# Linear attention and a hardswish layer on one core: the second chunk's features in two transfers, and three constants of the planner

## The chip, the core and the metric

The kernel runs on one core of a Trainium2 chip. The metric is device time of one execution in microseconds (us); of several runs the median is given. The engines are TensorE (PE; its weight loads are PEld), VectorE (DVE), ScalarE (ACT), GpSimd (POOL) and SyncE (SP), which here only issues transfers.

## The reference

```python
# r, k, v, w: (4, 8, 768, 48), u: (8, 48)
for t in range(S):
    cur = einsum('bhd,bhe->bhde', u * k_t, v_t)
    y[:, :, t] = einsum('bhd,bhde->bhe', r_t, state + cur)
    state = w_t[..., None] * state + einsum('bhd,bhe->bhde', k_t, v_t)
x = y.transpose(0, 2, 1, 3).reshape(3072, 384)
h = x @ w_in                          # 384 x 2048, given in float64
g = h * clip(h + 3, 0, 6) / 6
out = g @ w_out                       # 2048 x 384, given in float64
```

## The kernel before, in words

**Work.** The sequence is cut into 24 chunks of 128 tokens, and six blocks of four chunks. The recurrence of a chunk is turned into small matrix products; each finished block of 512 tokens then goes through the two large products. Block 0 does most of its large products directly; blocks 1 to 5 use a seven-product scheme for both of them.

**Steps of chunk i.** `feat{i}` fetches r, k and w side by side as one tile of 112 x 1545 values (`load_feat`), `tok{i}` fetches v. On DVE, `back{i}` scans w backwards (L372) and takes a reciprocal; `fore{i}` scans w forwards (L381); `K{i}` is k times the first scan (L392), `R{i}` is r times the second (L396), `own{i}` is r times k (L405). The two scans need only w. PE then does `dot{i}` (L415), `score{i}` (L440), `turn{i}` (a transpose, L456) and `kv{i}` (L536); ACT copies what `turn`, `dot` and `kv` left (`turned`, `sum`, `kvs`) and builds a diagonal (`diag0`, `diag1`, L431). `above{i}` merges the scores on DVE (L447), and `mid`, `decb`, `state`, `decay` carry the state on. In block 0, `first{i}` reads the last pair of heads on PE (L514, L523), `third{i}` copies it on ACT, `read{i}` does the rest on PE (L584, L514, L523), and `leave{i}` copies the result out on ACT. In later blocks `begin{i}` and `read{i}` take these places.

**Weights.** They arrive as float64. `fetch{j}` (j = 0 to 15, the first eight for w_in) brings 768 KB; ACT does `low{j}` and `whole{j}` (L340, L344), DVE does `shift{j}`, `join{j}` and `full{j}` (L349, L354, L359). `up0.f.c0` is a product of block 0 with w_in (L639) on two chunks, followed by `ramp` on ACT (L629) and `gate` on DVE (L650); `down0.c.q` is a product with w_out (L658) and needs `full{8+q}`. The steps `sin` and `sout` (L700, L712) make the sums of weights that the seven-product scheme needs; `up1.…` and `down1.…` are that scheme's products (L740, L791).

**What sets the order.** Every step is given to a planner (`plan.add`) with its engine, an assumed duration, the steps that it must follow, a due time ("key") and the buffers that it holds until named steps are done. The planner writes one fixed order for each engine from these; each engine then works through its order, and waits where something is late. `LAG` sets how long ahead of a block its chunks are due, `CONV` the due time of the first weight conversion and the distance from one to the next, `SUMS` the same for the sums. Three buffers hold features (`feat_in`), three hold raw weights (`bits`), two hold `more` and one holds `y_ps`, in which `kv`, `first` and `read` write.

**Start.** Until the first `up0.0.0` the planner puts "spins" on PE between steps: products of an identity whose result nobody reads (L1130), so many as fit into the time that it assumes PE would be idle.

Of the kernel before, what the change touches and what calls it, by code (L numbers as in the profile page):

```python
# [24 lines left out]
GBC = 3  # L25


LAG = 6.1
AHEAD = -3.5
LEAD = 2.5  # L30
BEHIND = (-1, -1, -1, 0, 6, 7)
# [1 line left out]
OWN = 0.07  # L33
SOLO = (0, 2, 3, 4, 5)
EARLY = 7
START = (-118.3, -135.2, -24.4, -60.3, -5.9, 13.2)
CONV = (-100.6, 7.2)
UP = (-68.7, 1.2, -9.3, 6.3)
SUMS = (52.1, 1.4)
LEAST = 2.0 ** -60  # L40

WORD_MIN, WORD_MAX = 1.125 * 2.0 ** -15, 1.875 * 2.0 ** 16
# [145 lines left out]
def fast_path(tc, feat, tok, wflat, ub, ug, moe_w_in, moe_w_out, out, flag, n_chunks):  # L188
# [5 lines left out]
    nc = tc.nc  # L194
# [13 lines left out]
    f64 = moe_w_in.dtype != F32  # L208

    with ExitStack() as ctx:  # L210
# [8 lines left out]
        chunk_of = [(i // NSEQ * 2 + i % 2) * n_chunks + i % NSEQ // 2 for i in range(NT)]  # L219
# [7 lines left out]
        plan = Plan()  # L227
        st = [dict() for _ in range(NT)]
# [8 lines left out]
        back = const.tile([PR, 2 * P, HL + 1], F32, name="back")  # L237
        starts = [const.tile([PR, 2 * P, HL + 1], F32, name=f"start_{i}") for i in range(2)]
        states = [const.tile([PR, P, D], F32, name=f"state_{i}") for i in range(2)]
        u_col = const.tile([PR, P, 2], F32, name="u_col")  # L240
# [37 lines left out]
        n = P * L  # L278
# [3 lines left out]

        def load_feat(i):
            a = io.tile([PR, nf], F32, name="feat_in")
            if i == 0:
                nc.sync.dma_start(out=a[:, 2 * n:], in_=feat[chunk_of[i], :, 2 * n:])
                nc.scalar.dma_start(out=u_col, in_=ug)
            else:
                nc.sync.dma_start(out=a, in_=feat[chunk_of[i]])
            st[i].update(a=a, r=a[:, :n].rearrange("q (x t) -> q x t", t=HL),  # L290
                         k=a[:, n:2 * n].rearrange("q (x t) -> q x t", t=HL), w=a[:, 2 * n:])

        def load_rest():
            nc.sync.dma_start(out=st[0]["a"][:, :2 * n], in_=feat[chunk_of[0], :, :2 * n])

        def load_u():
            nc.sync.dma_start(out=u_bc, in_=ub.to_broadcast([128, HD]))
# [569 lines left out]
        def do(fn, *args):  # L867
            return lambda: fn(*args)
# [5 lines left out]
        def when(i):  # L874

            bk, c = divmod(i, BC)
            return BASE[bk] - LAG - (BASE[bk] - BASE[bk - 1]) / BC * (BC - 1 - c) if bk else -99.0

# [6 lines left out]
        def scored(i):  # L885
            return f"score{i}" if i <= BC else f"read{i - 1}"

        def turned_by(i):
            return f"turn{i}" if i <= BC + 1 else f"begin{i - 2}"
# [4 lines left out]
        for i in range(NT):  # L894
            t = when(i)
            k = START[i] if i < len(START) else when(i - 2) - AHEAD
            first, last = is_first(i), is_last(i)
            dve = i < EARLY
            behind = [f"fetch{BEHIND[i]}"] if i < len(BEHIND) and BEHIND[i] >= 0 else []
            plan.add(f"feat{i}", "SP", 0.45 if i else 1.15, do(load_feat, i), behind + [f"feat{i - 1}"] * (i > 0) + ["later"] * (i == 1), k - 20, kb=690 if i else 231,  # L900
                     hold=[("feat", [f"K{i}", f"R{i}"] + [f"own{i}"] * (i < BY_PE))])
            plan.add(f"tok{i}", "SP", 0.45, do(load_tok, i), behind + [f"feat{i}"] * (i > 1) + ["later"] * (i < 2), k - 19.9, kb=197,
                     hold=[("tok", [f"read{i}"])])
            if i >= BY_PE:
                plan.add(f"rkt{i}", "SP", 0.45, do(load_rk, i), behind + [f"feat{i}"] * (i > 0), k - 19.8, kb=393,
                         hold=[("rk_in", [f"own{i}"])])
            plan.add(f"back{i}", "DVE", 1.4, do(back_scan, i), [f"feat{i}"] + [f"fore{i - 2}"] * (i > 1) + [f"back{i - 1}"] * (i > 0), k,
                     [("E", [f"K{i}", f"least{i}"])], port=True)
            plan.add(f"K{i}", "DVE" if dve else "POOL", 0.66 if dve else 1.32, do(make_k, i), [f"back{i}", f"least{i}"] + [f"K{i - 1}"] * (i > 0) + ["later"] * (i == 0),
                     k + 0.1, [("K", [scored(i), turned_by(i)])], port=True)  # L910
            plan.add(f"fore{i}", "DVE", 1.23, do(fore_scan, i), [f"back{i}"] + [f"fore{i - 1}"] * (i > 0), k + 0.2,
                     [("W", [scored(i), f"read{i}" if i < BC else f"begin{i}"])], port=True)
            plan.add(f"R{i}", "DVE" if dve else "POOL", 0.66 if dve else 1.32, do(make_r, i), [f"fore{i}"], k + 0.3,
                     port=True)
            plan.add(f"least{i}", "ACT", 0.2, do(least, i), [f"back{i}"], k + 0.2)
            if i < BY_PE:
                plan.add(f"own{i}", "DVE", 0.66, do(own, i), [f"feat{i}"] + ["later"] * (i == 0) + [f"own{i - 1}"] * (i > 0), k + OWN,
                         [("rk", [f"dot{i}"])], port=True)
                plan.add(f"dot{i}", "PE", 0.85, do(own_dot, i), [f"own{i}"], k + OWN, [("ps", [f"sum{i}"])])
                plan.add(f"sum{i}", "ACT", 0.22, do(own_sum, i), [f"dot{i}"], k + OWN, [("dg", [f"diag1{i}"])])  # L920
            else:
                plan.add(f"own{i}", "POOL", 2.0, do(own, i), [f"rkt{i}", "u"] + [f"own{i - 1}"] * (i > 0), k + 0.4,
                         [("rk", [f"sum{i}"])], port=True)
                plan.add(f"sum{i}", "DVE", 0.54, do(own_sum, i), [f"own{i}"], k + 0.5, [("dg", [f"diag1{i}"])])
# [3 lines left out]
            t = k + 1 if i < len(START) else t  # L928
# [52 lines left out]
                                 [f"leave{i - 1}", f"leave{i}"], when(i) - 50, kb=1, dmas=3)  # L981

        plan.add("u", "SP", 0.45, load_u, ["fetch3"], -60.0, kb=197)
        plan.add("later", "SP", 0.45, load_rest, ["feat0"], key=-999.0, kb=459)

        for j in range(len(pairs)):
            t = CONV[0] + j * CONV[1]
            plan.add(f"fetch{j}", "SP", 0.45, do(fetch, j), ["later"] * (j == 0), key=t - 20, kb=768 if f64 else 384,
                     hold=[("bits", [f"low{j}", f"join{j}"])] if f64 else ())
            if f64:  # L990
                plan.add(f"low{j}", "ACT", 0.9, do(low_scaled, j), [f"fetch{j}"], t, [("more", [f"full{j}"])])
                plan.add(f"whole{j}", "ACT", 0.84, do(low_whole, j), [f"low{j}"], t)
                plan.add(f"shift{j}", "DVE", 0.56, do(high_shift, j), [f"fetch{j}"], t, [("top", [f"full{j}"])], port=True)
                plan.add(f"join{j}", "DVE", 0.96, do(high_join, j), [f"shift{j}"], t, port=True)
                plan.add(f"full{j}", "DVE", 0.94, do(high_low, j), [f"join{j}", f"whole{j}"], t, port=True)
# [5 lines left out]
        for x, (c0, c1) in enumerate(parts):  # L1001
            m = c1 - c0
            for f in range(NFC):
                k = UP[2 * x] + f * UP[2 * x + 1]
# [7 lines left out]
        for c in classic:  # L1012
            for q in range(HF):
                k = D0 + c * D0 / BC + q * 1.29
# [9 lines left out]
        for n_, (s_, q) in enumerate((s_, q) for s_ in (1, 2, 4, 3) for q in range(0, HF, 2)):  # L1024
# [9 lines left out]
            if s_ in (2, 4) and q == 0:  # L1034
                before += [f"sin{s_ // 2}.{HF - 2}"]
            plan.add(f"sin{s_}.{q}", "DVE", 0.36, do(sum_in, s_, q), before, SUMS[0] + n_ * SUMS[1] / 4, hold, port=True)
        for n_, (t_, x) in enumerate((t_, x) for t_ in (1, 2, 4, 3) for x in range(2)):
# [3 lines left out]
            if t_ == 1 and x == 0:  # L1041
                before += [f"{ready}{len(pairs) - 1}"]
            plan.add(f"sout{t_}.{x}", "DVE", 0.95, do(sum_out, t_, x), before, SUMS[0] + 4 * SUMS[1] + n_ * SUMS[1] / 2,
                     [("bits", ["end"])] * (t_ != 3 and x == 0), port=True)
# [3 lines left out]
        for bk in range(NB):  # L1048
            K = BASE[bk]
# [67 lines left out]
        for k, (which, j) in enumerate(vets):  # L1117
            i = 8 + k // 2
# [255 lines left out]
def kernel(  # L1374
# [25 lines left out]
    flags = ctx.enter_context(tc.tile_pool(name="flags", bufs=1))  # L1400
    flag = flags.tile([1, 1], I32, name="flag")
    fast_path(tc, feat, tok, wflat, ub, ug, moe_w_in, moe_w_out, out, flag, n_chunks)
    bad = nc.values_load(flag[0:1, 0:1], min_val=0, max_val=128)
    with tc.If(bad > 0):
# [65 lines left out]
```

## Time and profile before

| | us |
|---|---|
| median of 6 runs | 574.91 (571.45 to 576.36) |
| the profiled execution | 571.62 |
| its span | 569.9 |
| first `up0.0.0` on PE | 32.0 |
| last product on PE ends | 564.6 |

The span is the time between the first and the last instruction that the profile has; the remaining 1.7 us of the execution lie around it. PE is busy for 558.0 us of it, DVE for 405.0, ACT for 273.6, POOL for 99.8. The 18 us that PE spent in spins count as busy. In the windows of the profile "PEclk" is the TensorE clock that was granted, as a share of full speed; in the timeline a bracket at the end of a row tells how long the engine was idle before it and which event ended that.

### The profile page before, as it was taken

The numbers are of one execution on the slowest core, as the hardware profiler recorded it, in microseconds if no ns is written. First come the engines' busy times: TensorE is split into PE (matmuls) and PEld (weight loads), VectorE is DVE, ScalarE is ACT, GpSimd is POOL, SyncE is SP. The second block draws the span as 40 slices with busy tenths as digits, with TensorE's granted clock in tenths as the row PEclk, the third lists the DMA queues.
The fourth block names the chain that finished last, engine by engine and source line by source line (L and its number), as shares of the span: only waits on it lengthen the run. The fifth ranks groups of instructions, "written<-read, shape, count | busy, mean of one in ns | idle before, by whom it ended". The sixth has DMA issues, their size and how long they took to land.

```text
span 569.9 us, 13575 instructions
## 1 busy us (share of the span) xinstructions
PE 558.0 (98%) x5636; PEld 500.9 (88%) x5636; DVE 405.0 (71%) x713; ACT 273.6 (48%) x724; POOL 99.8 (18%) x111
## 2 busy tenths in 40 slices
PE   8999899999999999999999999999999999999996
PEld 8888587689888999988999988999988999988996
DVE  7999989988687858677878767878656625255350
ACT  4688664643565633276633366633266611355100
POOL 2000000245513321223123133123122000000000
PEclk9999899999999999999999999999999999999998
DMA  8987822531613246930368360367100001000001
GB/s 273 279 276 232 266 67 64 158 110 44 181 55 99 78 125 203 252 89 12 123 214 266 98 168 8 127 205 220 41 16 2 9 1 36 29 1 1 1 15 47
DMA packets 23078, 63.98 MB, mean 112 GB/s; under 512 B 3120, under 2 KB 10352, under 8 KB 23008
## 3 DMA queue, kind: packets, MB, share of 16 engines
q1 hardware_dynamic: 22880, 63.02, 36.5%
q8 instruction: 46, 0.75, 0.6%
q14 instruction: 24, 0.20, 0.1%
q10 hardware_dynamic: 128, 0.00, 0.0%
HBM read 57.31 MB, written 4.72 MB: 109 GB/s over the span
## 4 chain that ended last, share of the span: by engine, by line
PE 94%; DVE 2%; DMA 2%; ACT 1%; issue 1%; SPq 0%; DVEq 0%; ACTq 0%
PE bankA L791 20%; PE bankA L740 18%; PE bankC L791 10%; PE bankC L740 9%; PE bankB L740 6%; PE bankB L791 5%; PE bankC L639 3%; PE bankA L639 3%; PE bankA L658 3%; PE y_ps L514 3%; PE y_ps L523 2%; PE y_ps L536 2%; PE ps L456 2%; DMA bits<-in_moe_w_in_dram 2%; PE bankB L440 2%; PE ps L415 1%
## 5 line engine op out<-in xcount | busy, mean ns | idle before, releaser
L749 ACT COPY g<-bankA 128x256 f32<-128x256 f32 x120 | 44.3, 371 | 58.7 <-PE bankA L740 56.7
L791 PE MATMUL bankA<-w_out,g 128*128 128x192 f32 x352 | 63.9, 328 | 0.0
L629 ACT ACTIVATE clip<-g,three 128x512 f32<-128x512 f32 x80 | 57.9, 723 | 7.9 <-DVE g L751 7.2
L740 PE MATMUL bankA<-xT,w_in 128*128 128x256 f32 x240 | 60.1, 382 | 0.0
L759 DVE SCALAR_TENSOR_TENSOR g<-clip,g 128x512 f32<-128x512 f32 x80 | 56.9, 712 | 2.6 <-ACT clip L629 2.4
L791 PEld LDWEIGHTS bankA<-w_out,g 128*128 128x128 f32 x352 | 57.9, 190 | 0.9
L804 ACT ACTIVATE o<-bankA 128x192 f32<-128x192 f32 x33 | 10.9, 330 | 88.8 <-PE bankA L791 88.8
L740 PEld LDWEIGHTS bankA<-xT,w_in 128*128 128x128 f32 x240 | 44.8, 190 | 6.0
L431 ACT ACTIVATE A<-eyes,dg 128x64 f32<-128x64 f32 x192 | 49.2, 336 | 0.4
L606 ACT COPY xT<-y_ps 48x256 f32<-48x256 f32 x80 | 29.3, 366 | 37.3 <-PE y_ps L523 36.4
L392 POOL TENSOR_TENSOR K<-feat_in,E 112x512 f32<-112x512 f32 x17 | 21.5, 1265 | 136.0 <-PE bankC L440 121.8
L740 PE MATMUL bankB<-xT,w_in 128*128 128x256 f32 x160 | 41.1, 379 | 0.0
L751 DVE TENSOR_TENSOR g<-bankB,g 128x256 f32<-128x256 f32 x40 | 16.9, 423 | 32.3 <-PE bankB L740 30.6
L396 POOL TENSOR_TENSOR W<-feat_in,W 112x512 f32<-112x512 f32 x17 | 23.1, 1357 | 87.2 <-DVE W L381 87.2
L751 DVE TENSOR_TENSOR g<-bankC,g 128x256 f32<-128x256 f32 x40 | 16.9, 421 | 27.3 <-PE bankC L740 27.2
L740 PEld LDWEIGHTS bankB<-xT,w_in 128*128 128x128 f32 x160 | 30.4, 190 | 4.1
L381 DVE TENSOR_TENSOR_SCAN W<-feat_in,start 112x520 f32<-112x520 f32 x24 | 30.6, 1274 | 3.1 <-PE y_ps L514 3.0
L372 DVE TENSOR_TENSOR_SCAN E<-feat_in,back 112x520 f32<-112x520 f32 x24 | 30.0, 1251 | 3.3 <-DMA feat_in<-in_feat_dram 3.1
L791 PE MATMUL bankA<-bits,g 128*128 128x192 f32 x176 | 30.3, 327 | 0.5 <-DVE o L806 0.5
L791 PE MATMUL bankB<-w_out,g 128*128 128x192 f32 x176 | 30.4, 326 | 0.0
L791 PEld LDWEIGHTS bankA<-bits,g 128*128 128x128 f32 x176 | 28.8, 190 | 0.9 <-DVE o L806 0.7
L791 PEld LDWEIGHTS bankB<-w_out,g 128*128 128x128 f32 x176 | 28.9, 190 | 0.0
(277 smaller groups left out, 1211.0 us busy)
## 6 DMA issues: line engine op xcount, KB each, us to landing
feat_in<-in_feat_dram SPq DMA_DIRECT2D x23, 675.9 KB, 5.9
bits<-in_moe_w_in_dram SPq DMA_DIRECT2D x8, 768.0 KB, 10.3
bits<-in_moe_w_out_dram SPq DMA_DIRECT2D x8, 768.0 KB, 4.8
feat_in<-in_moe_w_in_dram SPq DMA_DIRECT2D x8, 768.0 KB, 4.3
feat_in<-in_moe_w_out_dram SPq DMA_DIRECT2D x8, 768.0 KB, 4.2
rk_in<-in_tok_dram SPq DMA_DIRECT2D x15, 384.0 KB, 5.9
v_in<-in_tok_dram SPq DMA_DIRECT2D x24, 192.0 KB, 4.5
out_dram<-o SPq DMA_DIRECT2D x24, 192.0 KB, 2.1
```

The costliest lines, as they stand in the source:

```text
L372: nc.vector.tensor_tensor_scan(out=E_[:, ::-1], data0=d["w"][:, :0:-1], data1=back.rearrange("q p t -> q (p t)")[:, ::-1], initial=0.0, op ...
L381: nc.vector.tensor_tensor_scan(out=W_, data0=d["w"][:, :-1], data1=starts[i % 2].rearrange("q p t -> q (p t)"), initial=0.0, op0=ALU.mult, ...
L396: early(i).tensor_mul(d["R"], d["r"], d["R"])
L431: nc.scalar.activation(out=d["A"][:, h, :], in_=eyes, func=ACT.Copy, scale=d["dg"][:, h])
L606: nc.scalar.copy(out=blocks[bk]["xT"][g * GP:g * GP + D, :, at:at + HL], in_=st[i]["y_ps"][(g ^ a) * GP:(g ^ a) * GP + D, a, :, :])
L629: nc.scalar.activation(out=c[:, :m], in_=src, func=ACT.Relu, bias=three, scale=1.0)
L639: nc.tensor.matmul(h_ps[:, :(c1 - c0) * L], lhsT=w_in[:, f // 2, j, f % 2, :], rhs=b["xT"][:, j, c0 * L:c1 * L], start=(j == 0), stop=(j = ...
L740: nc.tensor.matmul(b["p", q, to][:, :HB], lhsT=w, rhs=rhs, start=(n == 0 and k in (1, 2, 5)), stop=(n == len(terms) - 1 and k in (2, 3, 4) ...
L749: nc.scalar.copy(out=to, in_=src)
L751: nc.vector.tensor_add(to, src, to)
L759: nc.vector.scalar_tensor_tensor(out=g, in0=b["r", q, p], scalar=6.0, in1=g, op0=ALU.min, op1=ALU.mult)
L791: nc.tensor.matmul(b["d", p, to][:, :h], lhsT=a, rhs=w(), start=(f == 0 and k in (1, 2, 5)), stop=(f == HF - 1 and k in (2, 3, 4)), skip_g ...
```

## The change

Chunk 1's features now come as chunk 0's do: w in a transfer of 228 KB, then r and k in one of 448 KB. `later0` and `later1` are these second transfers. `feat1` stands directly behind `later0` in SP's order, `later1` behind it; the values of chunks 0 and 1 (`tok0`, `tok1`) and the first weights (`fetch0`) wait for `later1` in the planner. `K1`, `R1` and `own1` need `later1`, and `R0` now names `later0`. The constants `LAG`, `CONV` and `SUMS` change, and with them the planned order of all engines.

```diff
-LAG = 6.1
+LAG = 7.5
-CONV = (-100.6, 7.2)
+CONV = (-100.6, 9.9)
-SUMS = (52.1, 1.4)
+SUMS = (52.1, 2.0)
...
         def load_feat(i):
             a = io.tile([PR, nf], F32, name="feat_in")
-            if i == 0:
+            if i < 2:
                 nc.sync.dma_start(out=a[:, 2 * n:], in_=feat[chunk_of[i], :, 2 * n:])
-                nc.scalar.dma_start(out=u_col, in_=ug)
+                if i == 0:
+                    nc.scalar.dma_start(out=u_col, in_=ug)
...
-        def load_rest():
-            nc.sync.dma_start(out=st[0]["a"][:, :2 * n], in_=feat[chunk_of[0], :, :2 * n])
+        def load_rest(i):
+            nc.sync.dma_start(out=st[i]["a"][:, :2 * n], in_=feat[chunk_of[i], :, :2 * n])
...
-            plan.add(f"feat{i}", "SP", 0.45 if i else 1.15, do(load_feat, i), behind + [f"feat{i - 1}"] * (i > 0) + ["later"] * (i == 1), k - 20, kb=690 if i else 231,
+            plan.add(f"feat{i}", "SP", 1.15 if i == 0 else 0.45, do(load_feat, i), behind + [f"feat{i - 1}"] * (i > 0) + ["later0"] * (i == 1), -500 if i == 1 else k - 20, kb=231 if i < 2 else 690,
...
-            plan.add(f"tok{i}", ... behind + [f"feat{i}"] * (i > 1) + ["later"] * (i < 2), k - 19.9, kb=197,
+            plan.add(f"tok{i}", ... behind + [f"feat{i}"] * (i > 1) + ["later1"] * (i < 2), k - 19.9, kb=197,
...
-            plan.add(f"K{i}", ... + ["later"] * (i == 0),
+            plan.add(f"K{i}", ... + [f"later{i}"] * (i < 2),
-            plan.add(f"R{i}", ..., do(make_r, i), [f"fore{i}"], k + 0.3,
+            plan.add(f"R{i}", ..., do(make_r, i), [f"fore{i}"] + [f"later{i}"] * (i < 2), k + 0.3,
-                plan.add(f"own{i}", ... + ["later"] * (i == 0) + ...
+                plan.add(f"own{i}", ... + [f"later{i}"] * (i < 2) + ...
...
-        plan.add("later", "SP", 0.45, load_rest, ["feat0"], key=-999.0, kb=459)
+        for i in range(2):
+            plan.add(f"later{i}", "SP", 0.45, do(load_rest, i), [f"feat{i}"], key=-999.0, kb=459)
...
-            plan.add(f"fetch{j}", ..., ["later"] * (j == 0), key=t - 20, ...
+            plan.add(f"fetch{j}", ..., ["later1"] * (j == 0), key=t - 20, ...
```

The order of the changed program, engine by engine, differs from the one before in these places (it can be read off without a run):

- SP: w0, rest0, **w1, rest1**, `tok1`, `tok0`, `fetch0` to `fetch2`, `feat2`, … Further on, `feat6` and `feat7` come before `fetch11` and `fetch13`.
- DVE at the start, before: `back0 fore0 own0 K0 R0 back1 own1 fore1 K1 R1 above0 shift0 join0 shift1 above1 join1 decb0`; after: `back0 fore0 own0 K0 back1 own1 fore1 K1 R1 R0 shift0 join0 above0 shift1 join1 above1 decb0`.
- PE at the start, before: `dot0 score0 turn0 dot1 kv0 turn1 score1 first0`; after: `dot0 turn0 dot1 kv0 score0 turn1 score1 first0`. There are 53 spins before and 54 after. Before, 11 of them stood between `score1` and `first0`; after, 4 stand ahead of `score1` and 7 behind it. From `first0` to `up0.0.0` both orders are the same.
- DVE behind `gate0.10.0`: `R2`, `decay2`, `decay3`, `above2`, `mid2`, `decb2`, `state2`, `above3` and what follows for chunks 2 and 3 come before `shift9`, `join9` and `full9`; before they came behind `full10`. `back4` to `K4` come before `shift10`, not behind `full13`. The last conversion, `full15`, comes behind `gate0.9.2`; before it came ahead of `gate0.3.2`.
- PE behind `up0.15.0`, before: `kv2 down0.0.0 down0.0.1 kv3 down0.0.2 score2 score3 first2 read2 down0.0.3 first3 down0.0.4 read3 down0.0.5 dot4 up0.0.2`; after: `score2 kv2 down0.0.0 score3 kv3 first2 read2 down0.0.1 dot4 first3 score4 turn4 read3 down0.0.2 up0.0.2`.
- PE at the start of block 1: before `begin8 read8 up1.0.1 …`; after `begin8 up1.0.1 …`, with `read8` 18 steps later. From there on both orders hold the same steps, with `begin`, `read` and neighbouring products moved by a few places.

More of the change, by code (lines that the diff above doesn't have):

```diff
@@ L899, in fast_path @@
             behind = [f"fetch{BEHIND[i]}"] if i < len(BEHIND) and BEHIND[i] >= 0 else []
-            plan.add(f"feat{i}", "SP", 0.45 if i else 1.15, do(load_feat, i), behind + [f"feat{i - 1}"] * (i > 0) + ["later"] * (i == 1), k - 20, kb=690 if i else 231,
+            plan.add(f"feat{i}", "SP", 1.15 if i == 0 else 0.45, do(load_feat, i), behind + [f"feat{i - 1}"] * (i > 0) + ["later0"] * (i == 1), -500 if i == 1 else k - 20, kb=231 if i < 2 else 690,
                      hold=[("feat", [f"K{i}", f"R{i}"] + [f"own{i}"] * (i < BY_PE))])
-            plan.add(f"tok{i}", "SP", 0.45, do(load_tok, i), behind + [f"feat{i}"] * (i > 1) + ["later"] * (i < 2), k - 19.9, kb=197,
+            plan.add(f"tok{i}", "SP", 0.45, do(load_tok, i), behind + [f"feat{i}"] * (i > 1) + ["later1"] * (i < 2), k - 19.9, kb=197,
                      hold=[("tok", [f"read{i}"])])
@@ L908, in fast_path @@
                      [("E", [f"K{i}", f"least{i}"])], port=True)
-            plan.add(f"K{i}", "DVE" if dve else "POOL", 0.66 if dve else 1.32, do(make_k, i), [f"back{i}", f"least{i}"] + [f"K{i - 1}"] * (i > 0) + ["later"] * (i == 0),
+            plan.add(f"K{i}", "DVE" if dve else "POOL", 0.66 if dve else 1.32, do(make_k, i), [f"back{i}", f"least{i}"] + [f"K{i - 1}"] * (i > 0) + [f"later{i}"] * (i < 2),
                      k + 0.1, [("K", [scored(i), turned_by(i)])], port=True)
@@ L912, in fast_path @@
                      [("W", [scored(i), f"read{i}" if i < BC else f"begin{i}"])], port=True)
-            plan.add(f"R{i}", "DVE" if dve else "POOL", 0.66 if dve else 1.32, do(make_r, i), [f"fore{i}"], k + 0.3,
+            plan.add(f"R{i}", "DVE" if dve else "POOL", 0.66 if dve else 1.32, do(make_r, i), [f"fore{i}"] + [f"later{i}"] * (i < 2), k + 0.3,
                      port=True)
@@ L916, in fast_path @@
             if i < BY_PE:
-                plan.add(f"own{i}", "DVE", 0.66, do(own, i), [f"feat{i}"] + ["later"] * (i == 0) + [f"own{i - 1}"] * (i > 0), k + OWN,
+                plan.add(f"own{i}", "DVE", 0.66, do(own, i), [f"feat{i}"] + [f"later{i}"] * (i < 2) + [f"own{i - 1}"] * (i > 0), k + OWN,
                          [("rk", [f"dot{i}"])], port=True)
@@ L983, in fast_path @@
         plan.add("u", "SP", 0.45, load_u, ["fetch3"], -60.0, kb=197)
-        plan.add("later", "SP", 0.45, load_rest, ["feat0"], key=-999.0, kb=459)
+        for i in range(2):
+            plan.add(f"later{i}", "SP", 0.45, do(load_rest, i), [f"feat{i}"], key=-999.0, kb=459)
         for j in range(len(pairs)):
             t = CONV[0] + j * CONV[1]
-            plan.add(f"fetch{j}", "SP", 0.45, do(fetch, j), ["later"] * (j == 0), key=t - 20, kb=768 if f64 else 384,
+            plan.add(f"fetch{j}", "SP", 0.45, do(fetch, j), ["later1"] * (j == 0), key=t - 20, kb=768 if f64 else 384,
                      hold=[("bits", [f"low{j}", f"join{j}"])] if f64 else ())
```

## The prediction

> **What bounds the kernel now.** The page comes first, then busy time and clock by stretches, then the chain that ended last, then the timeline of the start.
>
> ```profile
> span 569.9 us, 13575 instructions
> PE 558.0 (98%) x5636; PEld 500.9 (88%) x5636; DVE 405.0 (71%) x713; ACT 273.6 (48%) x724; POOL 99.8 (18%) x111
> ```
>
> PE is the bound, but its 558.0 us hold 18 us of spins. What can be won is the time before the first `up0.0.0`, the idle time of PE behind it, and time at a lowered clock. The stretches say where these lie:
>
> ```profile
> core 0: us, PE busy (x) PEld busy (x) DVE busy (x) ACT busy (x) POOL busy (x), PEclk, DMA share, GB/s
> 32.00:54.00 22.00, 22.00 (x113) 19.19 (x111) 20.26 (x35) 18.86 (x41) 0.00 (x0) 1.00 0.86 269
> 54.00:75.00 21.00, 18.93 (x308) 12.64 (x308) 20.18 (x35) 13.90 (x26) 0.00 (x0) 0.92 0.65 207
> 75.00:100.00 25.00, 24.06 (x328) 19.75 (x327) 22.05 (x40) 13.87 (x42) 0.00 (x0) 1.00 0.26 72
> 100.00:125.00 25.00, 25.00 (x350) 18.86 (x351) 23.03 (x40) 12.92 (x42) 7.37 (x5) 1.00 0.46 128
> 125.00:150.00 25.00, 23.87 (x294) 21.71 (x293) 20.90 (x37) 9.33 (x30) 13.86 (x13) 1.00 0.33 96
> 150.00:190.00 40.00, 40.00 (x357) 34.93 (x353) 30.35 (x54) 26.26 (x69) 11.71 (x12) 1.00 0.40 116
> ```
>
> PE stands idle for 2.07 us in 54 to 75, 0.94 in 75 to 100 and 1.13 in 125 to 150: 4.1 us. From 150 until the last stretches nothing is idle. DVE is nearly full until 125: a PE that runs ahead soon waits for DVE. The clock fell once:
>
> ```profile
> 62.00:63.00 1.00, 0.36 (x12) 0.18 (x8) 0.97 (x4) 0.45 (x2) 0.00 (x0) 1.00 0.98 297
> 65.00:66.00 1.00, 0.86 (x36) 0.69 (x26) 0.97 (x3) 0.57 (x1) 0.00 (x0) 0.52 0.63 55
> 66.00:67.00 1.00, 1.00 (x10) 0.59 (x3) 0.86 (x2) 0.96 (x3) 0.00 (x0) 0.50 0.66 227
> 67.00:68.00 1.00, 1.00 (x3) 0.58 (x2) 1.00 (x2) 0.96 (x3) 0.00 (x0) 0.50 1.04 424
> 68.00:69.00 1.00, 1.00 (x10) 0.18 (x8) 0.97 (x2) 0.22 (x1) 0.00 (x0) 0.78 0.88 232
> ```
>
> The clock lost 0.48 + 0.50 + 0.50 + 0.22 = 1.7 us, behind a stretch of small products with gaps. All that this change can remove behind the start is thus 4.1 + 1.7 = 5.8 us. The start, from the timeline and the chain:
>
> ```profile
> 1.73 0.43 SPq L289 DMA_DIRECT2D feat_in<-in_feat_dram  x1
> 9.70 1.24 DVE L372 TENSOR_TENSOR_SCAN E<-feat_in,back 112x520 f32<-112x520 f32 x1 [1.24 <-DMA feat_in<-in_feat_dram]
> ...
> 18.21 0.28 DVE S L469
> 18.54 0.32 PE y_ps L514 x4
> 19.27 0.96 PE bankA L1130 x6
> 23.16 2.28 PE bankA L1130 x16
> 30.47 1.55 PE bankA L1130 x12
> 32.02 1.30 PE bankC L639 x6
> ```
>
> DVE waits 1.24 us for chunk 1's single transfer, is then busy up to `decb0` (18.21), and that releases `first0` at 18.54. From there to 32.02 the chain is PE itself, spins included, without a gap.
>
> **The start, step by step.** Rest0's 448 KB, issued at 1.27, took 4.4 us and landed at 5.7. W1 stands right behind it; at the 240 GB/s at which rest0 followed w0 (448 KB from 3.8 to 5.7) its 228 KB land near 6.6, at the latest with the whole transfer of before, 9.6. DVE reaches `back1` behind `K0` at 7.85, so I take 7.85. `back1` and its reciprocal end at 9.3; `own1` needs rest1, which closes the same bytes as before, so about 9.6 again (8.5 to 10.2): a new wait of 0.3 us (0 to 0.9). Both DVE orders hold the same steps ahead of `decb0`, so `decb0` comes 1.24 - 0.3 = 0.9 us earlier, at 17.3 (17.0 to 17.9). But `R0` now ends behind `R1`, at 14.07 - 0.9 = 13.2, and `score0`, which ran at 8.84, waits for it. Behind it PE has `score0` 0.7, `turn1` 0.55, four spins 1.14, `score1` 0.7, seven spins 2.0 (0.285 each, from 2.28 for eight): with 0.1 of handing over `first0` starts at 18.4 less some overlap of neighbours, 18.2. So PE's own order, no longer DVE, sets `first0`, and **the start gains 0.35 us (-0.4 to 0.7)**, which the unchanged 13.48 us to `up0.0.0` pass on.
>
> Edits that I cost at nothing: SP's additional issue (0.41 to 0.44 us a piece) moves `tok1`, `tok0`, `fetch0` to `fetch2`, `feat2` and `tok2` back by 0.43. `low0` waited until 12.42 for `fetch0`, 9.24 us behind its issue, with 2.5 MB queued up to it; bytes set that, not issues. Uncovered it would be 0.43 us on ACT, where `diag1` has over 1 us of slack ahead of `above1`. `feat3` waits for `R0`'s buffer: 13.2, not 9.66. Its first reader is `back3` at 26.47, and such a transfer took 5.9 us. If that cover went, PE's spins would no longer hide it, and `dot3` would come late by the difference.
>
> [...]
>
> **54 to 72.** Up to `up0.15.0`, PE has no gap before and needs nothing later than before; it ends at 53.97 - 0.35 = 53.6. DVE passes `gate0.15.0` at 54.6 and then needs 0.7 (`above`) + 1.1 (`mid`, `decb`, `state`, 0.36 each) for chunk 2, 0.55 for `shift9`, 1.8 for chunk 3, 1.9 for `join9` and `full9`, 4.6 for `back4` to `K4` (1.45, 0.6, 1.2, 0.7, 0.7): `K4` at 65, `full10` at 68.4 (3.4 with `above4`). PE: `score2`, `kv2`, `down0.0.0`, `score3`, `kv3` to 57.0; `first2` waits for `kvs3` behind `low10` and `whole10` on ACT (0.92 + 0.84), 57.6; `read2` waits for `third2` as before (0.65). `low11` waits for `full9`'s `more` buffer until 60.5 and has `leave2` queued behind it on ACT, so `first3` comes at 63.5; `down0.0.1` and `dot4` lie between. `score4` waits for `K4` until 65; `read3` to 68.7, `down0.0.2` to 70.0; `leave3`, queued behind `low12`, which waits for `full10`, releases `up0.0.2` at 70.45. The new gaps are 0.6 + 0.65 + 0.9 + 0.5 = 2.65; but such sums by rows run short (the steps between 77 and 109 sum to 29.5 us and took 30.9 with no gap), and what PE needs more lies in front of these waits. I take 1.7 (1.0 to 4.2). Gone are the old 2.07. **Gain 0.35 here, and another 1.7 if the clock stays up.** It may fall again: between `down0.0.0` and `down0.0.1` lie 5.4 us of small products with 1.25 us of gaps; before, about 6 us with 1.9. I take it as up, narrowly.
>
> **75 to 150.** `full15` ends at 98.9 by the same walk, with DVE at the point where it was at 101.1 before. One gap is seen (`down0.0.6` for `full14`, 0.55) for the old 0.94: gain 0.4 (-1 to 0.9). `own8` and `sout1` come near 111 and 113 and are needed near 114 and 120. At the end `read8` no longer stands ahead of `up1.0.1`, which hides its wait for ACT (0.68), but `tx1.1` comes 0.9 behind `back11` where it had 2.2 of slack: gain 0.7 (-0.5 to 1.1). I take 0.35 off for waits at the sums, of which DVE has no slack to spare. Behind 150 both orders hold the same products with PE full: 0.
>
> **Sum.** 0.35 + 0.35 + 1.7 + 0.4 + 0.7 - 0.35 = 3.1 us. Against the profiled execution that is 571.62 - 3.1 = 568.5. The median of the runs shown is 3.29 us above it, so 574.91 - 3.1 = **571.8 us**. About 0.5%, 2.9 us, is what a measurement of this kernel can tell from no change.
>
> **Rivals.**
>
> *The lead is eaten (0.31).* The clock falls once more as before: 3.1 - 1.7 = 1.4, so 573.5. Or DVE, 20.18 of 21 and 23.03 of 25 busy, gives nothing more and only the start counts: 574.6. For it speaks that the gaps of chunks 2 and 3 look alike before and after; against it that 1.24 us of DVE waiting are gone and DVE gets its idle time in 75 to 110 back. Both are within 0.5%, as is the case that the split does nothing at all.
>
> *Slower: the conversions come too late for PE (0.23).* With `CONV` at 9.9 only two `down0.0` products are ready between the first steps of chunk 2 and the end of chunk 3, where five were. If `K4` and `full10` come over 1.5 us later than walked, PE's gaps reach 4.2 us and the clock falls in both stretches, at 1.7 each: 0.35 + 2.07 + 1.7 - 4.2 - 3.4 = -3.5, so 578.4. It decides from there on, since the old gaps at 93 and 145 stay.
>
> *Forecast (0.46):* clock up, gaps of 1.7: 571.8, itself 569.5 to 572.5.
>
> **Range and chances.** The lower end takes nearly all that can go, 5.8 + 0.35 = 6.1: 568.8. The upper end takes in most of the slower rival, up to 577.5; above it I leave 0.12, below 0.05. Faster 0.46, same 0.31, slower 0.23.
>
> **What would show it.** Right: `back1` at 7.9 with no wait for a transfer, `own1` near 9.7, `R0` near 13.2, `first0` near 18.2, `up0.0.0` near 31.7; PEclk at 1.00 throughout 54 to 75; less than 3 us idle in 54 to 150; the last product near 561.5. Wrong: `own1` behind 10.5 (rest1 late); granted clock under 0.95 in 54 to 75; PE waiting for L359 or L392 over 2 us in all; PE gaps behind 150, which would be `LAG`.

## The result, and the profile after

The changed kernel takes 578.12 us (median of 29 runs, 573.27 to 581.95), the kernel before 573.69 us (median of 66 runs beside them). The ratio is **1.0063, 95% interval 1.0046 to 1.008**: slower by 0.6%, where 571.8 us was forecast, about 0.5% faster than the 574.91 known then. The profiled execution took 577.13 us, its span is 575.4. The page begins with:

```profile
span 575.4 us, 13584 instructions
PE 561.6 (98%) x5638; PEld 503.4 (87%) x5638; DVE 405.5 (70%) x713; ACT 275.1 (48%) x724; POOL 112.8 (20%) x111
```

PE is busy for 3.6 us more with the same work, one spin (0.3 us) apart. The start, from DVE's timeline, came as walked:

```profile
7.91 1.24 DVE L373 TENSOR_TENSOR_SCAN E<-feat_in,back 112x520 f32<-112x520 f32 x1
9.19 0.21 DVE L377 RECIPROCAL start<-E 112x8 f32<-112x8 f32 x1
9.31 0.65 DVE L406 TENSOR_TENSOR rk<-feat_in 112x512 f32<-112x512 f32 x1
...
11.61 1.28 DVE L397 TENSOR_TENSOR W<-feat_in,W 112x512 f32<-112x512 f32 x2
```

No row ends in a bracket: DVE waits neither for w1 (`back1`, 7.91) nor for rest1 (`own1`, 9.31), and `R0`, the second of the two in the last row, ends at 12.9. In the chain that ended last, `first0` starts at 18.50 and `up0.0.0` at 31.82, 0.2 us earlier than before. The stretches behind it:

```profile
54.00:75.00 21.00, 19.17 (x338) 14.15 (x331) 18.49 (x33) 12.75 (x31) 0.00 (x0) 0.77 0.61 185
75.00:100.00 25.00, 25.00 (x296) 20.18 (x295) 21.40 (x38) 16.91 (x45) 1.18 (x1) 0.99 0.44 129
100.00:125.00 25.00, 24.88 (x228) 18.38 (x228) 23.64 (x42) 8.15 (x25) 11.65 (x3) 1.00 0.24 73
125.00:150.00 25.00, 21.84 (x355) 19.27 (x354) 17.98 (x31) 10.59 (x34) 12.42 (x12) 1.00 0.29 74
```

Two things stand out against before. The granted clock (the third number from the right) is 0.77 in 54 to 75, not 0.92. PE's idle time is 1.83 us there (2.07 before) and none in 75 to 100 (0.94), but 3.16 in 125 to 150 (1.13). The clock by the microsecond:

```profile
63.00:64.00 1.00, 1.00 (x3) 0.64 (x2) 1.00 (x2) 0.95 (x4) 0.00 (x0) 0.50 1.01 393
65.00:66.00 1.00, 1.00 (x9) 1.00 (x7) 1.00 (x3) 0.00 (x0) 0.00 (x0) 0.77 0.00 0
68.00:69.00 1.00, 1.00 (x9) 1.00 (x10) 0.27 (x1) 0.98 (x5) 0.00 (x0) 0.94 1.11 327
72.00:73.00 1.00, 1.00 (x2) 0.46 (x2) 1.00 (x2) 0.95 (x4) 0.00 (x0) 0.50 0.41 78
75.00:76.00 1.00, 1.00 (x4) 0.80 (x4) 0.00 (x0) 0.00 (x0) 0.00 (x0) 0.64 0.97 393
```

These are five rows of fourteen: there are two falls to one half, from 62 to 66 (1.7 us lost) and from 69 to 76 (3.4 us), where the profile of before had one of 1.7. The waits of PE in 125 to 150 show what the 3.16 us are:

```profile
PE bankC L792 <- DVE S__1533 L777: 1.3, 1, 1.3
PE bankB L792 <- DVE A L448: 1.0, 1, 1.0
PE bankA L792 <- DVE o L807: 0.5, 1, 0.5
PE bankA L792 <- ACT o L805: 0.4, 1, 0.4
```

The old wait of `read8` for ACT (0.7) is gone, but PE now waits for DVE: for a sum of the seven-product scheme (`S`, 1.3) and for an `above` step that has to free a bank (`A`, 1.0).

So much of the profile. A profile is one execution, and here that matters. Over single runs the time follows the granted clock (the changed kernel took 573.27 us at a mean clock of 0.995 and 581.95 at 0.98), so each run's time is split here into **time at full clock** (time x mean granted clock) and **clock lost** (the rest). For the 78 runs of before that stand beside the experiments the means are 568.7 and 6.0 us, for 30 runs of the changed kernel 570.5 and 7.0; runs over 1.5% above the fastest of the same kernel are left out. The mean clock is that of the whole span, so the clock lost also holds a fall behind PE's last product, which costs nothing (by the windows 1.6 us in the first profile of before, 0.7 in that of the changed kernel); differences of a few tenths in it mean nothing. The profiled run of before, at a clock of 0.994, lost only 3.4. It was a lucky one: none of the 78 had a higher clock.

### The profile page after: what moved, and what is told of

Same layout as the page of the kernel before. It is cut to its first block, busy times and chain, and to the rows that moved or that the text cites. A ratio compares the mean times of both kernels' runs of the same rounds, so it can differ in the third digit from the quotient of the medians.

```text
span 575.4 us, 13584 instructions
## 1 busy us (share of the span) xinstructions
PE 561.6 (98%) x5638; PEld 503.4 (87%) x5638; DVE 405.5 (70%) x713; ACT 275.1 (48%) x724; POOL 112.8 (20%) x111
## 4 chain that ended last, share of the span: by engine, by line
PE 94%; DVE 4%; ACT 1%; issue 0%; POOL 0%; DVEq 0%; POOLq 0%; ACTq 0%
PE bankA L792 19%; PE bankA L741 18%; PE bankC L792 10%; PE bankC L741 9%; PE bankB L741 6%; PE bankB L792 5%; PE bankA L659 4%; PE bankC L640 4%; PE bankA L640 3%; PE bankA L1132 3%; PE y_ps L515 2%; PE y_ps L537 2%; PE y_ps L524 2%; PE ps L457 2%; PE bankB L441 1%; PE ps L416 1%
## 5 line engine op out<-in xcount | busy, mean ns | idle before, releaser
L792 PE MATMUL bankA<-w_out,g 128*128 128x192 f32 x352 | 62.4, 327 | 0.4 <-ACT o L805 0.4
L741 PE MATMUL bankA<-xT,w_in 128*128 128x256 f32 x240 | 61.7, 382 | 0.0
L792 PEld LDWEIGHTS bankA<-w_out,g 128*128 128x128 f32 x352 | 58.0, 190 | 1.5 <-ACT o L805 0.7
L393 POOL TENSOR_TENSOR K<-feat_in,E 112x512 f32<-112x512 f32 x17 | 29.3, 1723 | 131.7 <-DVE E L373 92.6
L792 PE MATMUL bankA<-bits,g 128*128 128x192 f32 x176 | 31.0, 328 | 0.8 <-DVE o L807 0.8
L792 PE MATMUL bankB<-w_out,g 128*128 128x192 f32 x176 | 30.5, 327 | 1.0 <-DVE A L448 1.0
L792 PEld LDWEIGHTS bankA<-bits,g 128*128 128x128 f32 x176 | 28.8, 190 | 1.5 <-DVE o L807 1.4
L792 PEld LDWEIGHTS bankB<-w_out,g 128*128 128x128 f32 x176 | 28.8, 190 | 1.1 <-DVE A L448 1.1
```

The lines of the kernel that those rows point to most:

```text
L393: early(i).tensor_mul(d["K"], d["k"], d["E"][:, :, 1:])
L741: nc.tensor.matmul(b["p", q, to][:, :HB], lhsT=w, rhs=rhs, start=(n == 0 and k in (1, 2, 5)), stop=(n == len(terms) - 1 and k in (2, 3, 4) ...
L792: nc.tensor.matmul(b["d", p, to][:, :h], lhsT=a, rhs=w(), start=(f == 0 and k in (1, 2, 5)), stop=(f == HF - 1 and k in (2, 3, 4)), skip_g ...
```

## The experiments

**The split and the constants apart.** The first kernel keeps the split and takes the constants back, the second keeps the constants and takes the split back.

```diff
 split only (changed kernel with)      constants only (kernel before with)
-LAG = 7.5                             -LAG = 6.1
+LAG = 6.1                             +LAG = 7.5
-CONV = (-100.6, 9.9)                  -CONV = (-100.6, 7.2)
+CONV = (-100.6, 7.2)                  +CONV = (-100.6, 9.9)
-SUMS = (52.1, 2.0)                    -SUMS = (52.1, 1.4)
+SUMS = (52.1, 1.4)                    +SUMS = (52.1, 2.0)
```

> Only the split: the three constants are as before. Theory (the constants re-order the sparse stretch of chunks 2 and 3 and the sums, the split itself is harmless and worth the 0.2 us that up0.0.0 gained): up0.0.0 near 31.8, one half-clock stretch of 1.7 us in 54 to 75 as before (mean clock there 0.92), no spin of K8 over 3 us on POOL, time 573 to 574, a ratio of 0.997 to 1.001 to the kernel before. Rival (the split itself shifts DVE's work so that PE's gaps grow): clock in 54 to 75 at 0.80 or less, time 576 to 578, ratio over 1.004.

> Only the three constants: chunk 1 comes in one transfer as before. Theory (the constants cause the loss): as the changed kernel or slightly later: up0.0.0 at 32.0, two half-clock stretches, mean clock 0.77 to 0.80 in 54 to 75, over 3 us of PE idle in 125 to 150, ratio 1.005 to 1.009. Rival (the split causes it): clock 0.92 in 54 to 75, ratio within 0.002 of 1.

Split only: 572.22 us, **0.9948** (0.9922 to 0.9973), faster than expected. Constants only: 580.06 us, 1.006 (1.0026 to 1.0095), as expected, but for 2.7 us of idle time in 125 to 150 instead of over 3. The split is worth half a per cent, and the constants cost more than that. The split's gain is 0.4 us at full clock, the size of my start term, and 1.9 of clock lost (6.0 to 4.1). Why it loses less clock, its one profile can't tell: it has a fall at 28 to 32, behind which `up0.0.0` starts at 32.69, and one at 66 to 70, with 1.7 us lost in each.

**One constant taken back at a time, from the changed kernel.**

```diff
 e7: -LAG = 7.5            e8: -CONV = (-100.6, 9.9)   e9: -SUMS = (52.1, 2.0)
     +LAG = 6.1                +CONV = (-100.6, 7.2)       +SUMS = (52.1, 1.4)
```

> The changed kernel with LAG back at 6.1. Theory (CONV and SUMS cause the loss, LAG only the 0.18 and 0.38 us of PE idle in 190 to 236 and 362 to 408): 0 to 0.6 us faster than the changed kernel, ratio to before 1.004 to 1.008. Rival (LAG decides where the steps of chunks 2 to 6 stand among the products, and with it the gaps of 54 to 75 and of 125 to 150): ratio 0.995 to 1.000, gaps of 125 to 150 near 0.7.

> The changed kernel with CONV back at 7.2. Theory (later conversions thin out the products between the steps of chunks 2 and 3, so the clock falls for longer there): mean granted clock up from 0.988 to about 0.993 (3 us) and the late gap at down0.0.6 returns (0.9 us), the gaps of 125 to 150 stay at 2 to 3: 575 to 576 as the changed kernel's median less 2 to 3, ratio 0.999 to 1.003. Rival (SUMS does it all): ratio 1.005 to 1.008, clock unchanged.

> The changed kernel with SUMS back at 1.4. Theory (the sums, planned later and further apart, are what PE waits for in 125 to 150): PE idle there falls from 3.16 to about 1.1, which gives 2 us; the clock in the stretch of chunks 2 and 3 is as in the changed kernel (mean of the runs 0.986 to 0.989): ratio 1.002 to 1.004. Rival (the gaps of 125 to 150 come from LAG or CONV): gaps stay over 2.5, ratio 1.005 to 1.008.

**One constant moved at a time, from the split alone.**

```diff
 e11: -CONV = (-100.6, 7.2)   e12: -LAG = 6.1   e13: -SUMS = (52.1, 1.4)
      +CONV = (-100.6, 9.9)        +LAG = 7.5        +SUMS = (52.1, 2.0)
```

> The split with CONV alone at 9.9; LAG 6.1 and SUMS 1.4 as before. So far: the split alone 0.9948, with all three constants 1.0063, with CONV taken back 1.001, with LAG taken back 1.0105, with SUMS taken back 1.0175. Theory (late conversions are what hurts; LAG and SUMS at their later values only make room for them): the worst or next to the worst of all, ratio 1.012 to 1.025, with PE waiting 3 us or more for the above steps of a chunk on DVE between 125 and 190, and a mean granted clock of 0.982 to 0.987. Rival (the constants act each by itself, so that the effects add up: SUMS and LAG both help by themselves): ratio about 1.0063 + 0.0042 + 0.0112 = 1.022, which does not tell it apart from the first; it is told apart by the next two runs.

> The split with LAG alone at 7.5; CONV 7.2 and SUMS 1.4 as before. If the effects of the constants add up, LAG at 7.5 makes it faster by 0.4% (1.0063 against 1.0105), a ratio of 0.990 to 0.992. If LAG only makes room for late conversions, it gives nothing or costs its own gaps: 0.995 to 1.000, 0 to 2.5 us of idle time more behind 100.

> The split with SUMS alone at 2.0; LAG 6.1 and CONV 7.2 as before. If the effects add up, SUMS at 2.0 makes it faster by 1.1% (1.0063 against 1.0175), a ratio of 0.984 or so. If it only makes room for late conversions, it costs idle time: the split with LAG and SUMS both late gave 1.001 against 0.9948, of which I give SUMS the larger part: 0.997 to 1.001, idle in 125 to 150 at 1.5 to 2.5 for the 0.66 of the split alone.

With these, all eight combinations have been run, each with the split ("late" is the value of the changed kernel; ratios to before, in brackets the 95% interval; us are means of the runs, whose number stands at the end):

| late | ratio | at full clock | clock lost | runs |
|---|---|---|---|---|
| none (split only) | 0.9948 (0.9922, 0.9973) | 568.3 | 4.1 | 12 |
| CONV | 1.0136 (1.0096, 1.0176) | 571.0 | 10.2 | 6 |
| LAG | 1.0199 (1.0167, 1.023) | 575.7 | 8.6 | 6 |
| SUMS | 1.0055 (1.0024, 1.0087) | 571.0 | 5.8 | 10 |
| CONV, LAG | 1.0175 (1.015, 1.0201) | 573.7 | 10.5 | 5 |
| CONV, SUMS | 1.0105 (1.007, 1.014) | 572.8 | 8.2 | 6 |
| LAG, SUMS | 1.001 (0.9985, 1.0035) | 571.4 | 4.4 | 12 |
| all (changed kernel) | 1.0063 (1.0046, 1.008) | 570.5 | 7.0 | 30 |

Each constant moved alone makes the split slower. My expectations for taking LAG or SUMS back from the changed kernel were wrong, both theories of each: that costs, because the three stand or fall together. Those for LAG alone and SUMS alone were wrong in the same way. CONV went as its theories had it, taken back (1.001) and alone (1.0136), except that alone it made PE wait for an `above` step for only 0.6 us, not 3. Two readings hold. Clock lost is higher with the late CONV in all four pairs (by 6.1, 1.9, 2.4, 2.6), but only the last pair, 30 and 12 runs, and the first are clearly above their scatter. The others were run on different chips, on which before itself lost 4.9 and 6.4 us; measured against that, 0.4 and 0.8 are left of the 1.9 and 2.4. Time at full clock is made worse by LAG and SUMS where CONV stays (by 7.4, 2.7, 3.1 us), and by CONV alone (2.7). The greater part of this is idle time. With LAG alone it comes in 150 to 190:

```profile
125.00:150.00 25.00, 23.42 (x249) 21.34 (x247) 18.36 (x32) 7.29 (x25) 12.28 (x13) 1.00 0.23 69
150.00:190.00 40.00, 33.78 (x276) 28.61 (x277) 28.09 (x47) 21.52 (x59) 8.73 (x11) 0.91 0.34 104
```

That is 6.2 us idle in a stretch where the first profile of before had none, and the clock falls behind the first wait of it, from 152 to 159 (3.4 us lost). PE's longest waits there are 2.7 us for ACT's `kvs` and 2.6 us for ACT's `g`.

**More products where the clock falls.** If the clock falls because PE is too sparsely busy, idle products should hold it up.

```diff
+        def fill(to, n_):
+            for _ in range(n_):
+                nc.tensor.matmul(to[:, :L], lhsT=ident, rhs=ident, start=True, stop=True)
+
         def read_last(i):
+            if i >= 2:
+                to = bank("bankC")
+                fill(to, 2)
             new_y(i)
             read_state(i, (P - 1,))
             nc.tensor.drain()
             read_values(i, (P - 1,))
+            if i >= 2:
+                fill(to, 2)
```

These are eight products of the identity, four around `first2` and four around `first3`.

> The changed kernel with four more products of the identity with itself around first2 and four around first3 (their results are read by nobody; 8 x 0.285 = 2.3 us of PE at full clock), in a stretch where PE has gaps. Theory (the clock falls because PE is too sparsely busy there, and that is 3.4 of the 5.5 us of the span): granted clock over 0.95 in 54 to 75, 5.1 us of lost clock shrink to under 1.7, time down by 2 to 4 us against the changed kernel, 574 to 576, below or level with the kernel before. Rival 1 (the clock falls by some budget of power or of time, whatever PE does): clock stays at 0.75 to 0.80, time 578 to 580. Rival 2 (the clock is up but DVE is what sets the end of this stretch): clock up, up0.0.2 still near 74.35, time 577 to 578.

> The kernel before with the same eight added products around first2 and first3 (nobody reads their results). The 35 runs of before on the last chip have a mean granted clock of 0.988, from 0.971 to 0.994, while its one profile shows 0.994; that is 6.8 us lost on average. Theory (most of it falls in the sparse stretch of chunks 2 and 3, in before as in the changed kernel): mean clock 0.995 to 0.998 and 572 to 573, a ratio of 0.993 to 0.996. Rival (before loses its clock at the start, around 28 to 35, as the profiles of the split alone and of K8 on DVE do, and where nothing is filled): mean clock under 0.992, 575.5 to 577, ratio 1.000 to 1.003.

The changed kernel with the fill: 573.79 us, 0.9981 (0.9958 to 1.0005), against 1.0063 without. Its stretch:

```profile
54.00:75.00 21.00, 20.50 (x398) 15.91 (x397) 20.08 (x37) 14.86 (x37) 0.00 (x0) 1.00 0.61 198
```

The clock stays at 1.00 there. Over the whole span its mean is 0.9975, from 0.996 to 0.999 in 12 runs, for 0.988 without the fill. Clock lost goes from 7.0 to 1.4 us, and time at full clock up by 2.0 for the products: 3.6 us are won on balance by work that nobody reads. The kernel before with the same fill takes 574.11 us, 0.9981 (0.9962 to 1.0), less than expected: clock lost falls from 6.0 to 3.2 and no further. Its profile has no fall in 54 to 75 but one of 7 us from 29 to 36 (3.4 us lost), where nothing was filled. So both theories held a part there.

> The split alone with two products of the identity ahead of first2 and two ahead of first3, and none behind (nobody reads their results; 4 x 0.285 = 1.1 us, of which some 0.7 lies in idle time, as the 54 to 75 stretch of the four-product version showed). Theory (the clock falls because PE is too sparsely busy, and a little is enough): no fall in 54 to 75, mean clock 0.995 or more for the 0.993 of the split alone, 571 to 572, ratio 0.990 to 0.994. Rival (half of the fill is not enough): clock 0.993, 572.5 to 573.5, ratio 0.995 to 0.997.

The split alone with the two products ahead and none behind: 575.34 us, 1.0039 (1.0014 to 1.0063), slower than without them, as neither theory had it. Its profile has a fall from 64 to 72, with 3.4 us lost, twice the 1.7 of the shortest falls, and clock lost is 6.0 for 4.1. Half of the fill did not hold the clock here, and time at full clock is 569.5 for 568.3. A little fill is no remedy that can be counted on.

**A step that looked like the culprit.** In the changed kernel one row of POOL stands out: `K8`, 2.58 us long before, now takes 9.86 us, beside DVE's sums of w_out, which stand back to back on DVE from 115.3 on.

```profile
114.69 9.86 POOL L393 TENSOR_TENSOR K<-feat_in,E 112x512 f32<-112x512 f32 x1 [7.19 <-PE bankA L659]
```

```diff
-            early(i).tensor_mul(d["K"], d["k"], d["E"][:, :, 1:])
+            (nc.vector if i == 8 else early(i)).tensor_mul(d["K"], d["k"], d["E"][:, :, 1:])
```

> The changed kernel with K8 on DVE instead of POOL, nothing else moved. Theory (K8 is held for 9.86 us by DVE's seven sums without a pause, and PE's 3.2 us of gaps in 125 to 150 come from that): K8 takes 0.7 us on DVE, PE idle in 125 to 150 falls to about 1.1, time down by 1.5 to 2.1 us, 576.0 to 576.6; clock in 54 to 75 unchanged at 0.77. Rival (the gaps come from the later conversions and sums, K8 only waits beside them): gaps of 125 to 150 stay at 2.5 to 3.5, time within 0.7 us of the changed kernel, or up by 0.7 for the step that DVE now has to do.

On DVE it takes 0.68 us:

```profile
123.91 0.68 DVE L393 TENSOR_TENSOR K<-feat_in,E 112x512 f32<-112x512 f32 x1
```

It stands behind the sums there and ends at 124.6, as on POOL (124.55), while PE reaches the same gaps 1.3 us earlier in this run (the one for `A` ends at 131.84, not 133.12). So `K8` came 1.3 us later as PE sees it, and PE's idle time in 125 to 150 is 3.17 us as before, with the same four waits: 577.59 us, 1.0034 (1.0007 to 1.0061), 570.8 at full clock for 570.5. My theory falls: `K8` is not what PE waits for. That the gaps belong to the order of DVE's steps behind it is what remains, and is argued. The clock in 54 to 75, expected at 0.77, was 1.00 in this profile.

**The same two kernels once more, for their profiles.**

> The kernel before once more, unchanged, for a second profile: its one profile shows 0.994, its 80 other runs a mean of 0.988 to 0.991. Theory (the clock falls at three places, around 28 to 35, 62 to 72 and less often behind, each time for 3.4 or 6.9 us, and which of them it takes differs from run to run; the profiled run of before was one with a single fall): falls at 28 to 35 or a longer one in 62 to 72, at no place that PE is densely busy; clock 0.985 to 0.991. Rival (the falls are tied to the kernel's order and are the same in every run): one fall at 65 to 69 again, 0.994.

> As the run before this one: a third profile of the kernel before. Theory: places and lengths differ from those of the other two profiles. Rival: the same.

> The changed kernel once more, unchanged, for a second profile. Theory: falls at 28 to 35 in some runs, and one or two in 62 to 76; PE idle time in 125 to 150 at 3.16 again, since that belongs to the order and not to the clock. Rival (the idle time of 125 to 150 follows from the clock falls before it): idle there differs by over 0.5 us.

> As the run before this one: a third profile of the changed kernel. Theory: falls differ in place and length, idle in 125 to 150 again 3.16. Rival: falls the same, or idle different.

The second profile of before (582.63 us) has falls from 13 to 20 (3.4 us lost) and, for 20.5 us, from 67 on (10.2 lost): a place and a length that its theory did not have. The third (575.84 us) has three falls where the first had one:

```profile
30.00:31.00 1.00, 1.00 (x24) 0.86 (x17) 1.00 (x2) 0.75 (x4) 0.00 (x0) 0.50 0.55 58
66.00:67.00 1.00, 0.88 (x36) 0.67 (x39) 1.00 (x2) 0.14 (x1) 0.00 (x0) 0.71 0.30 37
67.00:68.00 1.00, 1.00 (x25) 0.85 (x18) 0.97 (x2) 0.98 (x2) 0.00 (x0) 0.50 0.67 132
97.00:98.00 1.00, 1.00 (x4) 0.36 (x2) 0.96 (x3) 0.00 (x0) 0.00 (x0) 0.56 0.04 6
98.00:99.00 1.00, 1.00 (x33) 0.89 (x32) 0.42 (x2) 0.47 (x1) 0.00 (x0) 0.50 0.02 6
```

The changed kernel's second profile (574.23 us) has none in 54 to 75, only one at 29 to 33; its third (578.46 us) has that one and both of 63 to 67 and 70 to 77. So the same program takes its falls at different places, as the theory had it. The theory's other part, that they spare dense work, fails: the fall at 97 comes while PE works without a gap (its busy time is 1.00 in every microsecond from 95 to 109). The idle time does not vary with the falls in the changed kernel's second profile:

```profile
54.00:75.00 21.00, 18.82 (x384) 14.29 (x383) 20.17 (x37) 14.95 (x36) 0.00 (x0) 1.00 0.63 199
125.00:150.00 25.00, 21.83 (x387) 19.39 (x381) 19.91 (x34) 10.69 (x35) 12.44 (x11) 1.00 0.36 101
```

With a clock of 1.00 in 54 to 75, PE is idle for 3.17 us in 125 to 150 again. In the third it is 2.71, and the missing 0.45 stands in 150 to 190, where the falls have pushed it.

## Why the prediction was wrong

**The start: right.** `back1` at 7.91 (7.85 forecast), `own1` at 9.31 with no wait (9.6), `R0` done at 12.9 (13.2), `first0` at 18.50 (18.2), `up0.0.0` at 31.82 (31.7). The gain is 0.2 us, not 0.35: `score0` starts only at 13.59, behind `kv0` and one more spin, not behind `R0`. The second transfer was not late: it had landed by 9.31, where the single one had come at 9.70. From issue to landing w0 and rest0 took 2.9 and 4.0 us (3.0 and 4.4 before), w1 5.5 and rest1 6.8; with issues at 1.73 and 2.20, w1 landed at 7.2 (6.6 forecast) and rest1 at 9.0 (9.6).

**54 to 72, the gaps: right.** 1.83 us, 1.7 forecast, though the rows summed to 2.65 and the 1.7 was a judgement; the two waits of 0.6 and 0.65 came as walked. In the second profile, with the clock up, `up0.0.2` starts at 71.64; there the stretch began 0.9 us later, behind a fall at 29 to 33, so that the forecast 70.45 was right to 0.3 us.

**54 to 72, the clock: the first step that failed.** I took it as up, for 1.7 us; it fell for 5.1 in the first profile, so that `up0.0.2` started at 74.35. My reason was PE's gaps, 1.25 against 1.9 us in some 6 us. But the gaps came as forecast and the clock fell for longer, and in the second profile PE was idle for more (2.18 us) and the clock did not fall at all. So the gaps were the wrong condition. The rival that had two falls made them depend on gaps of 4.2 us, which did not come either; that its 578.4 us lie next to the measured 578.12 is luck. What did change is the dense work. Of the `down0.0` products, the longest of this stretch, half are left between 54 and 75. The first row is the kernel before, the second the changed one, the third its second profile (PE's busy time in that line, its rows, the clock):

```profile
54.00:75.00 21.00, 10.28 (x24) 0.92 0.65 207
```

```profile
54.00:75.00 21.00, 7.41 (x12) 0.77 0.61 185
```

```profile
54.00:75.00 21.00, 4.67 (x12) 1.00 0.63 199
```

Six products of four rows have become three; the busy times can't be compared, since they are longer where the clock is lower: in the changed kernel's first profile the four rows of `down0.0.0` took 1.56 us from 54.84 on, at a clock of 1.00, and those of `down0.0.2` 2.93 us from 71.63 on, at 0.50. The prediction names this ("only two `down0.0` products are ready … where five were") and then prices only the gaps. That the late CONV costs clock is shown by two of its four pairs (6.1 and 2.6 us more lost), and that less of it is lost with eight more products in this stretch is shown by the fill (7.0 to 1.4 us, and 6.0 to 3.2 in the kernel before). That the missing `down0.0` products are the link is argued, and they don't decide it alone, as the third row shows. Over the profiles without a fill the link shows only as a tendency. With the late CONV (8 to 12 such rows) five of eight lost 5.1 us or more between 60 and 90, one 1.7 and two nothing. With the old one (18 to 24 rows) two of seven lost that much, four 1.7 and one nothing; SUMS alone, with 20 rows, has a fall of 10 us.

**The offset between profile and median: a failure beside it.** I carried the 3.29 us from the profiled 571.62 to the median as a constant. They are mostly falls that this one run did not have: 6.0 us lost in the mean, 3.4 in it. The forecast 1.7 us were thus 1.7 of a larger and varying number, and the mean change is 1.0 us of clock lost more.

**75 to 150, the waits at the sums: the second step that failed.** The gap at 93 is gone altogether (0.94 us won, where I took 0.4). For 125 to 150 I summed 0.7 gained and 0.35 lost for waits at the sums. The 0.7 came, since the wait for ACT is gone; the 0.35 became 2.7 us of waits for DVE and ACT on L792 beyond the one for `o` that before had too (0.5). I had `own8` and `sout1` on time by a walk that ended at 120, and did not walk DVE's `above` and sums behind it. That the conversions' delay is paid there is in part so: with CONV taken back, 1.9 us of the 3.16 stay, and 0.35 come in 150 to 190.

**Behind 150: nearly right.** 0.6 us of new gaps up to 408, none forecast. LAG was meant to show there; LAG late alone shows what it does without the others.

**The sum.** At full clock I had forecast a gain of 1.45 us, all terms but the clock; the changed kernel is 1.8 us slower: 0.2 won at the start, 1.5 lost in idle time on the whole (5.9 for 4.4 in the first profiles behind 54), the rest not assigned. That is 3.2 us from the forecast, most of it in 125 to 150, where 0.8 us of idle time were forecast and 3.16 came. The clock was to give 1.7; clock lost adds 1.0 in the mean of all runs, which is 2.7 us from the forecast. So the two steps that failed weigh about the same. The measured 1.8 and 1.0 make 2.8 us; the ratio, 3.6 us by runs beside each other, has an interval from 2.6 to 4.6. How much of it is clock remains uncertain by about 1 us, and why one run falls where another doesn't is open.

**The better version** is the split with the old constants: 572.22 us, 0.9948 to before (1.0063 for the changed kernel).

## What to carry to other kernels

Where a kernel's runs differ by their granted clock, split the time into a part at full clock and the clock lost before you argue from one profile; that profile may be the luckiest of them. A due time for one kind of step can't be judged alone: here every one of three constants, moved by itself on top of the split, cost 1 to 2.5%, and the moved set still cost more than the old one. That shorter gaps keep the clock up needs a run before it enters a sum: here PE's gaps in 54 to 75 were 1.83 us with the clock at 0.77 and 2.18 us with it at 1.00.

## What the runs showed of the hardware that I had not expected

In these runs the clock fell to one half, for about 3.4 us or a multiple of that. The 18 profiles have 37 falls ahead of PE's last product, all with rows of 0.50 in their middle: 21 lost 1.7 us, 13 lost 3.4, two 5.1 and one 10.2, which at one half are 3.4, 6.8, 10.2 and 20.5 us. In the first profile of before it is one of 1.7 (0.52, 0.50, 0.50, 0.78 in four rows), in that of the changed kernel one of 1.7 and, from 69 to 76, one of 3.4. One program has its falls at different places in different runs: 65 in one profile of before, 29, 66 and 97 in another.

No long wait of PE stands ahead of the falls in the first profiles: in the kernel before its longest one from 54 to 69 is 0.65 us, in the changed kernel from 54 to 76 too. With the eight small products more (8 x 0.285 = 2.3 us at full clock) the clock was 1.00 in 54 to 75, as it was in the changed kernel's second profile without them; the mean clock was 0.9975 over 12 runs with them, 0.988 over 30 without.

An elementwise product on POOL (`K8`) took 9.86 us beside DVE's two-input sums back to back, while the other 16 of its kind on POOL took 1.2 us in the mean. That the sums hold it up was not tested; it cost nothing here, since PE's idle time in 125 to 150 was the same (3.17 us) with `K8` on DVE.
